# Two attention and MLP layers on one core: the loads of the head on another queue, a second tile centred, the first key product in two parts, and new orders

## The chip, the core and the metric

The kernel runs on one core of one Trainium2 chip. The metric is the device time of one execution in microseconds (us). The same program is timed several times, and the median counts. One execution is also recorded by the hardware profiler.

The core has a matrix engine (TensorE; PE in the profile for the products, PEld for loading the stationary operand), three engines for elementwise work (VectorE is DVE, ScalarE is ACT, GpSimd is POOL) and SyncE (SP), which here only starts transfers. ACT and POOL can start transfers too. Each engine works through its own list of instructions in order, and semaphores make one wait for another.

## What is computed

The input x is 2048 tokens of 512 channels. Two kinds of blocks follow each other twice, each with a residual sum:

```python
x = x + A(layernorm(x))      # linear attention, 32 heads of 16 channels
x = x + B(layernorm(x))      # MLP
# A(x): q, k, v = split(x @ wqkv);  phi(t) = where(t > 0, t + 1, exp(t)) + 1e-6
#   kv = sum over tokens of phi(k) v^T, z = sum over tokens of phi(k), per head
#   out = (phi(q) @ kv) / (phi(q) . z + 1e-6);  return out @ wo
# B(x): y = layernorm(x);  return gelu(y @ w1 + b1) @ w2 + b2      # 512 -> 1792 -> 512
```

Data and weights are bfloat16; the weights are the same in both layers.

## The kernel before

The tokens are cut into 16 tiles of 128 and four chunks of four tiles. A program in Python makes a graph of named operations (class `Graph`). Five lists written out by hand, `CONF["ORDER"]`, one per engine, then set the order in which every engine works through its operations (`Settled.run`, L144). `CONF["PLACES"]` says which slot of which pool (PSUM banks, SBUF buffers) each tile of data takes, and so which earlier user it has to wait for. `CONF["WAY"]` says on which engine some operations run. `assign_waits` (L186) turns the graph into semaphore waits. So the order of the work is that of the lists; the planned durations in the code decide nothing on the chip.

Names, with the layer or tile number behind them:

- Loads: `x0`, `x1` (chunk 0), `xc1` to `xc3` (chunks 1 to 3), `wk0`, `wk1` (two halves of the key weights), `wq`. `CONF["LOADS"]` names each load's queue (L711 to L716). `wv`, `wo`, `w1`, `w2` are loaded by POOL's queue once all transposes of the first norms are done.
- Norm of tile t in block A or B of layer L (`norm`, L757): `stats`, `aggr`, `veps`, `pow` (reciprocal root, on POOL), `nmr`, `norm`. Two tiles of the head have other forms: with `cen` the tile is only centred (`cenA0_0`, L789), goes through TensorE transposes early (`PTC0`, then `tcC0` copies it), and the missing factor is applied as the scale of the exponential (`expk0_0`, `reluk0_0`). With `stat3` set to "act", tile 3 gets its sums from ACT (`sumA0_3`, `sqA0_3`).
- Transposes: `TA`, `TB`, `TP` are DMA transposes issued by SP (L812, L1080); `PTA` with `tcA` are done by TensorE and copied by ACT. In the kernel before, tiles 1, 2 and 3 of the first norm use TensorE (`PTA0_1` to `PTA0_3`).
- Attention: `K`, `Q` (four products of 128 x 512 each), `exp`, `relu`, `min`, `phi` for the feature map, `Z` and `G` (sums over tokens; G is the product of the normed tile with phi(k)), `KV`, `M` (joined with wo), `D`, `ln`, `rec`, `pr`, `pz`, `red`, `den` (denominators), `WO` and `RA` (output and residual sum).
- MLP: `W1`, `gelu`, `W2`, `b2`, `RB` (residual sum). In the last layer `RB1` writes a bfloat16 row block into an output buffer and SP stores it (`OD`). The last tile is done in two halves: columns 0 to 383 (`W21_15_h0`, `RB1_15_0`, `OD15_0`) and 384 to 511 (`W21_15_h1` and so on).

TensorE starts with products on constants (`warm`), while the first loads are under way.

The output buffers are two slots of `outb` (L657). There are ten slots of `yb` for normed tiles and eight of `pkb` for phi(k) (L620).

`attn_k` can already split the key product in two: `halves` (L874) reads the setting `ks`, and with it the parts (2, 3) and (0, 1) of the contraction become two operations, each waiting only for its own half of the weights. No tile of the kernel before sets it.

Of the kernel before, what the change touches and what calls it, by code (L numbers as in the profile page):

```python
# [6 lines left out]
BF16 = mybir.dt.bfloat16  # L7
ACT = mybir.ActivationFunctionType
ALU = mybir.AluOpType

P = 128
# [174 lines left out]
def assign_waits(graph, order, sems, dma_sems):  # L186
# [10 lines left out]
    while len(done) < total:  # L197
        moved = False
        for e in ENGINES:
# [43 lines left out]
    LOADS=[['x0', 'sp', 'x', 0, 0, 1, ''], ['x1', 'sp', 'x', 0, 1, 4, ''], ['wk0', 'sp', 'wk', 0, 0, 2, ''], ['wk1', 'act', 'wk', 0, 2, 4, 'ones'], ['xc1', 'act', 'x', 1, 0, 4, 'x0'], ['xc3', 'act', 'x', 3, 0, 4, ''], ['wq', 'act', 'wq', 0, 0, 4, ''], ['xc2', 'act', 'x', 2, 0, 4, '']],  # L243
    ORDER={
# [39 lines left out]
        "act":  # L284
# [1064 lines left out]
```

## Time and profile before

| | us |
|---|---|
| median of 3 runs | 325.99 (325.9 to 327.17) |
| the profiled execution | 326.31 |
| its span, first to last instruction | 325.1 |
| PE busy | 316.7 (97%) |
| DVE / ACT / POOL busy | 219.3 / 188.9 / 134.9 |
| mean granted TensorE clock | 0.999 |

The profiled execution's time is 1.2 us longer than its span. A busy PE is counted from the first to the modelled end of pipelined products, so idle time of PE is a better sign than its share. The "chain" of the profile goes back from the last instruction, at each step to what released it. Line numbers are those of the kernel before. Landing records and DMA records are the trace's own lists of when each transfer's pieces ran and when its semaphore was raised.

### The profile page before, as it was taken

To read this page: it belongs to the slowest core of one execution; us is meant where nothing else is said; L and a number is where in the kernel's file an instruction comes from. 1 tells how busy PE (TensorE), PEld (TensorE's weight loads), DVE (VectorE), ACT (ScalarE), POOL (GpSimd) and SP (SyncE) were. 2 spreads that over 40 slices of the span, in tenths; PEclk is the share of its full clock that TensorE was granted. 3 is DMA by queue.
4 is the path that set the end of the run, shared out by engine and by line. 5 is a ranking of instruction groups with operands and counts; after the bars stand their busy time and mean duration, and the time that the engine had idled before them with its cause. 6 is when DMAs were issued, how large, how long until landed. Compare 5 with 4: busy or idle time off the path is not lost.

```text
span 325.1 us, 4707 instructions
## 1 busy us (share of the span) xinstructions
PE 316.7 (97%) x1673; PEld 157.2 (48%) x1703; DVE 219.3 (67%) x536; ACT 188.9 (58%) x324; POOL 134.9 (42%) x208
## 2 busy tenths in 40 slices
PE   7899999998999999999999999999999999999997
PEld 3344554665454444444444444558544444444443
DVE  6987799989897496029349899999886843101103
ACT  4799658586675125875982277969824442653220
POOL 6562768793146045001421503976685454000000
PEclk9999999999999999999999999999999999999999
DMA  7734595224011403202101110131143322301002
GB/s 252 188 63 91 139 387 138 43 57 81 11 38 35 90 10 72 49 0 49 34 0 32 34 32 0 26 73 36 33 82 83 69 41 56 79 0 34 16 32 65
DMA packets 51779, 21.55 MB, mean 66 GB/s; under 512 B 46956, under 2 KB 50284, under 8 KB 51756
## 3 DMA queue, kind: packets, MB, share of 16 engines
q1 hardware_dynamic: 49468, 14.18, 20.1%
q0 software_dynamic: 1056, 4.72, 4.2%
q10 hardware_dynamic: 1232, 2.36, 2.2%
q8 instruction: 13, 0.21, 0.3%
q14 instruction: 10, 0.08, 0.1%
HBM read 8.00 MB, written 2.10 MB: 31 GB/s over the span
## 4 chain that ended last, share of the span: by engine, by line
PE 87%; DVE 4%; ACT 3%; DMA 3%; issue 1%; POOL 1%; SPq 0%
PE ps L1177 28%; PE ps L1140 27%; PE ps L879 8%; PE ps L1110 7%; PE ps L896 6%; PE ps L971 4%; PE ps L1000 3%; PE ps L909 2%; DVE xsb L1115 1%; DMA wqkv<-in_A_wqkv_dram 1%; DMA t<-yb 1%; DVE stats L775 1%; PE ps L1163 1%; ACT L1303 1%; ACT gT L1145 1%
## 5 line engine op out<-in xcount | busy, mean ns | idle before, releaser
L1145 ACT ACTIVATE gT<-ps,b1c 128x512 bf16<-128x512 f32 (+1 forms) x140 | 77.2, 601 | 67.2 <-PE ps L1140 66.8
L1140 PE MATMUL ps<-t,w 128*128 128x512 bf16 (+1 forms) x552 | 102.3, 336 | 1.5 <-issue 1.1
L1177 PE MATMUL ps<-w,gT 128*128 128x512 bf16 x425 | 97.6, 379 | 0.5
L1140 PEld LDWEIGHTS ps<-t,w 128*128 128x128 bf16 x560 | 54.6, 98 | 45.5 <-ACT gT L1145 1.6
L1177 PEld LDWEIGHTS ps<-w,gT 128*128 128x128 bf16 x434 | 42.5, 98 | 50.2
L847 ACT ACTIVATE eb<-ps 128x512 bf16<-128x512 f32 x63 | 36.8, 608 | 30.3 <-PE ps L879 15.9
L784 POOL TENSOR_TENSOR rstd<-veps,neghalf 128x1 f32<-128x1 f32 x64 | 38.5, 610 | 22.4 <-DVE veps L782 20.3
L1187 DVE TENSOR_TENSOR outb<-ps,xsb 128x512 bf16<-128x512 f32 x15 | 10.3, 689 | 44.5 <-PE ps L1177 40.1
L879 PE MATMUL ps<-wqkv,t 128*128 128x512 bf16 x125 | 30.6, 379 | 2.2 <-DMA t<-yb 1.1
L775 DVE BATCH_NORM_STATS2 stats<-xsb 128x6 f32<-128x512 f32 x48 | 32.4, 682 | 0.2
L1110 PE MATMUL ps<-gtb,t 128*128 128x512 bf16 x124 | 30.4, 379 | 0.2
L858 ACT ACTIVATE rb<-ps 128x512 bf16<-128x512 f32 x44 | 26.1, 608 | 3.7 <-PE ps L896 2.1
L782 POOL TENSOR_SCALAR veps<-mv 128x1 f32<-128x1 f32 x34 | 7.6, 224 | 48.0 <-DVE mv L777 44.0
L1076 POOL TENSOR_TENSOR t<-t,rr 128x512 bf16<-128x512 bf16 x18 | 19.9, 1114 | 11.3 <-DVE rr L1072 7.6
L798 ACT ACTIVATE yb<-xsb,nmr,rstd 128x512 bf16<-128x512 f32 x21 | 16.9, 811 | 12.9 <-POOL nmr L795 12.5
L896 PE MATMUL ps<-wqkv,t 128*128 128x512 bf16 x95 | 23.6, 379 | 0.1
L1183 DVE TENSOR_TENSOR xsb<-ps,xsb 128x512 f32<-128x512 f32 x16 | 10.8, 679 | 14.7 <-PE ps L1177 14.7
L879 PEld LDWEIGHTS ps<-wqkv,t 128*128 128x128 bf16 x128 | 12.1, 97 | 16.9 <-ACT yb L798 1.5
L1110 PEld LDWEIGHTS ps<-gtb,t 128*128 128x128 bf16 x128 | 12.4, 98 | 14.5 <-issue 0.3
L1064 POOL TENSOR_TENSOR lr<-t,zrow 128x512 f32<-128x512 bf16 x13 | 14.9, 1153 | 9.9 <-ACT zrow L984 3.7
L1126 DVE TENSOR_TENSOR xsb<-xsb,b2b 128x512 f32<-128x512 f32 x20 | 14.4, 730 | 5.2 <-ACT yb L798 5.2
L803 DVE TENSOR_SCALAR yb<-xsb,mv,rstd 128x512 bf16<-128x512 f32 x27 | 15.1, 566 | 3.1 <-POOL rstd L784 2.1
(100 smaller groups left out, 362.1 us busy)
## 6 DMA issues: line engine op xcount, KB each, us to landing
w<-in_B_w_dram POOLq DMA_DIRECT2D x4, 896.0 KB, 9.7
out_dram<-outb SPq DMA_DIRECT2D x15, 128.0 KB, 2.0
t<-in_A_x_dram ACTq DMA_DIRECT2D x3, 512.0 KB, 4.1
t<-yb SPq DMA_TRANSPOSE x61, 2.5
wqkv<-in_A_wqkv_dram ACTq DMA_DIRECT2D x1, 512.0 KB, 5.2
wqkv<-in_A_wqkv_dram POOLq DMA_DIRECT2D x1, 512.0 KB, 4.5
wo<-in_A_wo_dram POOLq DMA_DIRECT2D x1, 512.0 KB, 5.6
t<-in_A_x_dram SPq DMA_DIRECT2D x1, 384.0 KB, 3.1
```

Of the source, the lines that this page charges most:

```text
L775: G.op("dve", lambda e: e.bn_stats(stats[:, s.slot, :], src()), 620, reads=src_keys, writes=[k + "s"], tiles=[s, *src_tiles], name=f"stats ...
L784: G.op("pool", lambda e: e.tensor_tensor(rstd[:, s.slot:s.slot + 1], veps[:, s.slot:s.slot + 1], neghalf[:], op=ALU.pow), 570, reads=[k + ...
L798: G.op("act", lambda e: e.activation(yb[:, y.slot, :], src(), ACT.Identity, bias=nmr[:, s.slot:s.slot + 1], scale=rstd[:, s.slot:s.slot + 1]),
L847: G.op("act", lambda e: e.activation(eb[:, et.slot, :], bank(bt), ACT.Exp, scale=by()), 478, reads=[src_key, *more_keys], writes=[f"e{tag} ...
L858: G.op("act", lambda e: e.activation(rb[:, rt.slot, :], bank(bt), ACT.Relu, scale=by()), 478, reads=[src_key, *more_keys], writes=[f"r{tag ...
L879: ins = e.matmul(bank(b), lhsT=yTa(yT)[:, dt, k * P:(k + 1) * P], rhs=wqkv[:, dt, D:2 * D], start=(i == 0 and n == 0), stop=(i == len(part ...
L896: ins = e.matmul(bank(b), lhsT=yTa(yT)[:, dt, k * P:(k + 1) * P], rhs=wqkv[:, dt, 0:D], start=(dt == 0), stop=(dt == DT - 1))
L1076: lambda e, d=d, tok=tok, heads=heads: e.tensor_tensor(heads(tok()), heads(tok()), rr[:, d.slot, :].unsqueeze(2).broadcast_to([P, H, DH]), ...
L1110: ins = e.matmul(bank(wb), lhsT=yTa(pq)[:, kt, k * P:(k + 1) * P], rhs=gtb[:, kt, :], start=(kt == 0), stop=(kt == DT - 1))
L1140: ins = e.matmul(bank(b, n), lhsT=w1[:, dt, ft * P:(ft + 1) * P], rhs=yTa(yT)[:, dt, k0 * P:k1 * P], start=(dt == 0), stop=(dt == DT - 1))
L1145: G.op("act", lambda e, ft=ft, b=b, k0=k0, k1=k1, n=n: e.activation(gT[:, g.slot, ft * 512 + k0 * P:ft * 512 + k1 * P], bank(b, n), ACT.Ge ...
L1177: ins = e.matmul(bank(b), lhsT=gT[:, g.slot, ft * 512 + k * P:ft * 512 + (k + 1) * P], rhs=w2[:, ft, :], start=(ft == 0), stop=(ft == FT - 1))
```

## The change

Settings, orders and buffers change; the arithmetic does not.

- `LOADS`: `xc3`, `wq` and `xc2` are issued by SP instead of ACT. On SP they stand behind `x0 x1 wk0 TA0_0` (with `TA0_1` between `wq` and `xc2`). `wk1` and `xc1` stay with ACT.
- `cen1`: tile 1 is centred too and goes through TensorE transposes as `PTC1`, `tcC1`. Its normed form, used by Q and G, is transposed by DMA (`TA0_1` on SP), in place of `PTA0_1`, `tcA0_1`.
- `ks0`: the first key product becomes `K0_0a` (halves 2, 3 of the weights, from `wk1`) and `K0_0b`.
- The last layer's outputs use the ten slots of `yb`; `outb` goes, and `pkb` grows from 8 to 10 slots.
- All five orders and all places are written anew. `W21_15_h0` and `RB1_15_0` now come before `W21_15_h1` and `RB1_15_1`, with `RB1_10` still between the two additions.
- `WAY`: in layer 0, `b20_0` to `b20_2` go from POOL to DVE and `b20_7` to `b20_13` from DVE to POOL; in layer 1, `b21_1`, `b21_3`, `b21_4` go to POOL, `b21_0`, `b21_13` to DVE; some 20 `pr` and `pz`, some 30 `veps` and four `za` change sides between DVE and POOL, among them `pz0_1_0` to POOL, `vepsA0_0` and `vepsA0_2` to DVE.

```diff
-    LOADS=[..., ['xc3', 'act', 'x', 3, 0, 4, ''], ['wq', 'act', 'wq', 0, 0, 4, ''], ['xc2', 'act', 'x', 2, 0, 4, '']],
+    LOADS=[..., ['xc3', 'sp', 'x', 3, 0, 4, ''], ['wq', 'sp', 'wq', 0, 0, 4, ''], ['xc2', 'sp', 'x', 2, 0, 4, '']],
         "sp":
-            "x0 x1 wk0 TA0_0 TA0_4 TA0_5 TA0_7 TA0_13 TA0_6 TA0_12 TA0_14 TA0_15 TA0_8 TA0_9 TA0_10 TA0_11 b1 Tb1 b2 TP0_1_3 "
-            "TP0_1_1 TP0_1_0 TP0_1_2 TB0_0 TB0_1 TB0_2 TB0_3 TB0_7 TP0_2_1 TB0_6 TB0_4 TB0_5 TP0_2_0 TP0_2_2 TP0_2_3 TA1_0 "
...
-            "OD15_1 OD10 OD15_0",
+            "x0 x1 wk0 TA0_0 xc3 wq TA0_1 xc2 TA0_4 TA0_5 TA0_7 TA0_6 TA0_13 TA0_12 TA0_14 TA0_15 TA0_8 TA0_10 TA0_9 TA0_11 "
+            "b1 Tb1 TP0_1_3 TP0_1_1 TP0_1_0 TP0_1_2 TB0_0 TB0_1 b2 TB0_2 TB0_3 TP0_2_1 TB0_4 TB0_7 TB0_5 TB0_6 TP0_2_2 "
...
+            "OD11 OD12 OD8 OD9 OD15_0 OD10 OD15_1",
         "pe":
-            "warm0 warm7 warm6 warm5 PTC0 warm4 warm3 warm2 warm8 warm1 K0_0 PTA0_2 PTA0_1 K0_2 PTA0_3 K0_1 G0_0_0 K0_3 "
-            "Q0_0_2 Q0_0_0 K0_4 Q0_0_1 G0_1_0 G0_2_0 K0_5 G0_3_0 K0_7 Z0_0 G0_4_0 K0_13 K0_6 Q0_1_3 Q0_1_0 G0_5_0 Q0_1_2 "
...
-            "W21_11_7 W21_8_7 W21_9_0 W21_9_7 W21_10_7 W21_15_h1 W21_15_h0",
+            "warm0 warm8 warm4 warm7 warm5 PTC0 warm3 warm2 warm6 warm1 K0_0a K0_0b PTC1 PTA0_2 K0_1 PTA0_3 K0_2 G0_0_0 K0_3 "
+            "G0_1_0 Q0_0_2 Q0_0_1 Q0_0_0 K0_4 Q0_1_0 K0_5 G0_2_0 G0_3_0 G0_4_0 K0_7 Q0_1_3 K0_6 Z0_0 G0_5_0 K0_13 Q0_1_2 "
...
+            "W21_8_7 W21_9_0 W21_9_7 W21_10_7 W21_15_h0 W21_15_h1",
         "act":
-            "wk1 xc1 sumA0_3 tcC0 xc3 sqA0_3 wq tcA0_2 expk0_0 tcA0_1 reluk0_0 expk0_2 tcA0_3 expk0_1 xc2 reluk0_1 expk0_3 "
+            "wk1 xc1 sumA0_3 tcC0 sqA0_3 expk0_0 tcC1 tcA0_2 reluk0_0 expk0_1 tcA0_3 reluk0_1 expk0_2 reluk0_2 reluk0_3 "
...
         "dve":
-            "ones statsA0_0 aggrA0_0 cenA0_0 statsA0_2 aggrA0_2 statsA0_1 aggrA0_1 vepsA0_1 normA0_2 normA0_0 normA0_1 "
+            "ones statsA0_0 aggrA0_0 vepsA0_0 cenA0_0 statsA0_2 normA0_0 aggrA0_2 statsA0_1 vepsA0_2 aggrA0_1 cenA0_1 "
+            "vepsA0_1 normA0_2 statsA0_4 normA0_3 mink0_0 normA0_1 aggrA0_4 phik0_0 statsA0_7 mink0_1 statsA0_5 phik0_1 "
...
-        NT4, NYB, NPK, NER, NGT, NLR, NSTAT, NOUT = 12, 10, 8, 4, 2, 2, 12, 2
+        NT4, NYB, NPK, NER, NGT, NLR, NSTAT = 12, 10, 10, 4, 2, 2, 12
...
-        outb = SB("outb", [P, NOUT, D], BF16)
...
-                ot = Tile(OUT, f"out{st}")
-                G.op("dve", lambda e: e.tensor_tensor(outb[:, ot.slot, :], bank(b), xsb[:, st, :], op=ALU.add), 600,
+                ot = Tile(YB, f"out{st}")
+                G.op("dve", lambda e: e.tensor_tensor(yb[:, ot.slot, :], bank(b), xsb[:, st, :], op=ALU.add), 600,
```

In the part of TensorE's order between the first attention and the first MLP, `Q0_3_1` no longer stands ahead of `KV0_0`, nor `Q0_3_0` ahead of `WO0_0_0`; `Q0_2_3` does instead. Three Q products rather than two stand between the `WO0` products. Before the first product on chunk 1 (`W10_1`), `W10_0_8_1` and `W10_0_11_1` are new; they stood some units later.

More of the change, by code (lines that the diff above doesn't have):

```diff
@@ L242 @@
     WARM=[[512, 512, 512, 512, 512, 512, 512], [256], [256], [256], [256], [256], [256], [256], [256]],
-    LOADS=[['x0', 'sp', 'x', 0, 0, 1, ''], ['x1', 'sp', 'x', 0, 1, 4, ''], ['wk0', 'sp', 'wk', 0, 0, 2, ''], ['wk1', 'act', 'wk', 0, 2, 4, 'ones'], ['xc1', 'act', 'x', 1, 0, 4, 'x0'], ['xc3', 'act', 'x', 3, 0, 4, ''], ['wq', 'act', 'wq', 0, 0, 4, ''], ['xc2', 'act', 'x', 2, 0, 4, '']],
+    LOADS=[['x0', 'sp', 'x', 0, 0, 1, ''], ['x1', 'sp', 'x', 0, 1, 4, ''], ['wk0', 'sp', 'wk', 0, 0, 2, ''], ['wk1', 'act', 'wk', 0, 2, 4, 'ones'], ['xc1', 'act', 'x', 1, 0, 4, 'x0'], ['xc3', 'sp', 'x', 3, 0, 4, ''], ['wq', 'sp', 'wq', 0, 0, 4, ''], ['xc2', 'sp', 'x', 2, 0, 4, '']],
     ORDER={
         "sp":
[38 rows of a table removed]
-        "act":
[31 rows of a table removed]
-        "dve":
[42 rows of a table removed]
-        "pool":
[16 rows of a table removed]
[38 rows of a table added]
+        "act":
[30 rows of a table added]
+        "dve":
[42 rows of a table added]
+        "pool":
[16 rows of a table added]
     },
@@ L671, in build_kernel @@
         STATS = Pool("stats", NSTAT)
-        OUT = Pool("out", NOUT)
         psum = Pool("psum", 8)
@@ L1168, in mlp_down @@
                          tiles=[hb, g], name=f"W2{L}_{st}_h{h}", lat=MM_DRAIN, n=FT)
-                    G.op("dve", lambda e, hb=hb, cs=cs, n=n: e.tensor_tensor(outb[:, ot.slot, cs], bank(hb, n), xsb[:, st, cs], op=ALU.add),
+                    G.op("dve", lambda e, hb=hb, cs=cs, n=n: e.tensor_tensor(yb[:, ot.slot, cs], bank(hb, n), xsb[:, st, cs], op=ALU.add),
                          60 + n * 1.06, reads=[f"w{L}_{st}_{h}", ("x", st)], writes=[f"out{st}_{h}"], tiles=[hb, ot], name=f"RB{L}_{st}_{h}", lat=60)
-                    dma("sp", lambda e, cs=cs: e.dma_start(rows(out_dram, c)[:, k, cs], outb[:, ot.slot, cs]), [f"od{st}_{h}"],
+                    dma("sp", lambda e, cs=cs: e.dma_start(rows(out_dram, c)[:, k, cs], yb[:, ot.slot, cs]), [f"od{st}_{h}"],
                         tiles=[ot], reads=[f"out{st}_{h}"], name=f"OD{st}_{h}", sem=f"d_out_h{h}", kb=n // 4)
@@ L1185, in mlp_down @@
             else:
-                ot = Tile(OUT, f"out{st}")
-                G.op("dve", lambda e: e.tensor_tensor(outb[:, ot.slot, :], bank(b), xsb[:, st, :], op=ALU.add), 600,
+                ot = Tile(YB, f"out{st}")
+                G.op("dve", lambda e: e.tensor_tensor(yb[:, ot.slot, :], bank(b), xsb[:, st, :], op=ALU.add), 600,
                      reads=[f"w{L}_{st}", ("x", st)], writes=[f"out{st}"], tiles=[b, ot], name=f"RB{L}_{st}", lat=40)
-                dma("sp", lambda e: e.dma_start(rows(out_dram, c)[:, k, :], outb[:, ot.slot, :]), [f"od{st}"], tiles=[ot],
+                dma("sp", lambda e: e.dma_start(rows(out_dram, c)[:, k, :], yb[:, ot.slot, :]), [f"od{st}"], tiles=[ot],
                     reads=[f"out{st}"], name=f"OD{st}", sem=("out", ot), kb=128)
```

514 rows, old and new, of tables (ORDER, PLACES, WAY) are left out of this document.

## The prediction

> **What bounds the kernel now.** I read the page's shares first, then busy time by stretches, then the chain that ended last, then the timelines of the places where TensorE stands still. TensorE bounds it:
>
> ```profile
> PE 316.7 (97%) x1673; PEld 157.2 (48%) x1703; DVE 219.3 (67%) x536; ACT 188.9 (58%) x324; POOL 134.9 (42%) x208
> PE 87%; DVE 4%; ACT 3%; DMA 3%; issue 1%; POOL 1%; SPq 0%
> ```
>
> The second line is the chain's share by engine. The change adds and removes no matrix product (TA0_1's four PE transposes become PTC1's four). So only TensorE's gaps, its end and new gaps can move the time. Busy time by stretch (us: PE, PEld, DVE, ACT, POOL, clock, DMA share, GB/s) shows where they are:
>
> ```profile
> 6.00:9.00 3.00, 2.44 (x16) 1.26 (x17) 2.67 (x10) 1.79 (x5) 1.97 (x6) 1.00 0.98 326
> 12.00:15.00 3.00, 1.94 (x10) 0.73 (x9) 3.00 (x13) 2.39 (x4) 2.00 (x5) 1.00 0.87 232
> 15.00:18.00 3.00, 3.00 (x14) 1.36 (x15) 2.70 (x9) 1.95 (x4) 1.67 (x7) 1.00 0.22 44
> 76.00:80.00 4.00, 3.27 (x26) 2.35 (x24) 4.00 (x7) 2.40 (x6) 0.36 (x1) 1.00 0.56 101
> ```
>
> TensorE is full from 15 us on, at full clock, but for one hole before 80. In order of time, the chain names what ends last (start, us, what):
>
> ```profile
> 1.71 4.47 DMA wqkv<-in_A_wqkv_dram
> ...
> 10.60 4.26 DMA t<-yb
> ...
> 79.41 1.02 issue
> ```
>
> K0_0 waits for wk0 (6.18), K0_4 for the transpose TA0_4 (14.86), and W10_1_5_0 stands at 79.4. From here each 512-column product costs 0.216 us by its weight loads (K0_3 to Q0_0_2: 0.86 for four); I call four a unit.
>
> **The head, first tiles.** In the new order DVE puts vepsA0_0 (0.15) ahead of cenA0_0 (4.19 before, now 4.26), so tcC0 on ACT ends at about 5.75 instead of 5.63. K0_0a needs only wk1, landed at 5.78 by the landing records: it starts at 5.82, K0_0b at 6.25 (wk0 6.18), and K0_0 is done at about 6.87 instead of 7.28. expk0_0, at 8.04 because ACT first sat behind PTA0_2 (idle 1.21), starts at 6.93. cenA0_1 (0.35, the row of cenA0_0) is the added DVE work; its cover is gone, since DVE is 2.67 of 3 busy there, and normA0_2 slips from 6.43 to 7.03. PTC1 follows at 6.9, tcC1 at 7.5 to 8.1 behind expk0_0, so K0_1 starts at 8.16, where K0_2 started at 8.20. Then PTA0_3 (0.26) at 9.02, K0_2 at 9.28, G0_0_0 at 10.14, K0_3 at 11.0. Up to here nothing is won but G0_1_0's input: reluk0_1 ends at 11.0, phik0_1 at 11.46, against 14.26 before, because both first tiles now come early. So G0_1_0 runs at 11.87 and Q0_0_2 at 12.73.
>
> **The moved loads.** ACT gains nothing from losing them: with xc3's issue between tcC0 and sqA0_3, these start 0.49 us apart, the usual pitch.
>
> ```profile
> 5.04 0.60 ACT L835 ACTIVATE t<-ps 128x512 bf16<-128x512 bf16 x1
> 5.04 0.33 ACTq L702 DMA_DIRECT2D t<-in_A_x_dram  x1
> 5.50 0.39 ACTq L708 DMA_DIRECT2D wqkv<-in_A_wqkv_dram  x1
> 5.53 0.71 ACT L770 ACTIVATE eb<-t,stats 128x512 bf16<-128x512 bf16 x1
> ```
>
> On SP they stand behind waits. TA0_0 now issues at 5.6 (normA0_0 moves up) and takes 1.28 of SP; xc3 then goes at 6.95 and wq at 7.35 (0.4 each, instead of 5.04 and 5.50). TA0_1 waits for normA0_1 (about 8.9) and goes at 9.0; behind it xc2 at 10.3; behind that TA0_4, which waits for normA0_4 (about 11.9). 512 KB moved in about 1.6 us of full DMA share (xc3's packets 6.5 to 8.2). So xc3 moves about 8.0 to 9.6, wq to 11.3, TA0_1's 128 KB to 12.2 (landed 12.7), xc2 to 13.8, TA0_4 to 14.7 (landed 15.2). x tiles 8 to 15 are read later than that; wq is needed at 12.73. Q0_0_2 therefore meets TA0_1 on the spot.
>
> K0_4 comes after Q0_0_1 and Q0_0_0, at 15.33. It started at 14.99 with two units fewer done. The gain is 2 x 0.864 - 0.38 = 1.35 us if TA0_4 has landed by then. No row shows a transpose queued behind a load on its own queue, so I bound it: alone a transpose takes 2.5 us (61 of them), beside loads on the other queue 4.1 to 4.3. With 4.3 from 11.93, TA0_4 lands at 16.2 and the gain is 0.4; with 2.5 it lands at 14.4 and the gain stays 1.35. I take 1.1, near the upper end, because xc2 is issued 1.6 us ahead of TA0_4 instead of 0.23.
>
> [...]
>
> Does the lead survive? ACT is 3.00 of 3 busy from 18 to 21 and DVE from 21 to 24, but ACT idles 2.6 us and DVE 4.8 us in all between 15 and 38, mostly waiting for TensorE. Following banks and queues in the new order, K0_5 needs TA0_5 (about 16.4, used at 17.1) and K0_11 comes at about 32.6 instead of 33.7. I carry -1.1.
>
> **To the first MLP.** One Q unit fewer stands ahead of WO0_0 and one more behind it; pz0_1_0 (0.69) goes from DVE to POOL, where 1.13 us of idle time before pr0_0_3 takes most of it. So the residual sums start earlier still, and ten units of PE cover the way to TB0_1 instead of nine. Cost 0; if POOL were late here, up to 0.7.
>
> **The hole at 79.** W10_1_5_0 waits for TB0_5, issued at 76.02, which takes 4.3 us instead of 2.5. The DMA records show why: a 16 KB packet of the instruction queue occupies one engine from 77.93 for 1.36 us, and the last sixteenth of TB0_5 lands at 80.34. The hole is 1.36 us of TensorE. In the new order W10_0_8_1 and W10_0_11_1 (0.44 each) stand ahead of the first W10_1, and the last transpose is TB0_6, about as late as TB0_5 was. [...] Gain between 0 and 1.36; I take 0.9.
>
> [...]
>
> **The rest.** b20, b21, pz, pr and veps change sides; over the whole DVE program the kinds I count by median pitch fall from 201 to 199 us, and TensorE's units per stage are the same or one apart. Before, TensorE loses three further waits of 0.2 to 0.4 us (at 194, 208 and 217); new ones of that size will come. I charge 0.2, between -0.5 and +1.5.
>
> **The end.**
>
> ```profile
> 321.33 0.29 DVE L1169 TENSOR_TENSOR outb<-ps,xsb 128x128 bf16<-128x128 f32 x1 [1.92 <-DMA out_dram<-outb]
> 321.80 0.69 DVE L1187 TENSOR_TENSOR outb<-ps,xsb 128x512 bf16<-128x512 f32 x1 [0.18 <-DMA out_dram<-outb]
> 322.69 0.56 DVE L1169 TENSOR_TENSOR outb<-ps,xsb 128x384 bf16<-128x384 f32 x1 [0.20 <-PE ps L1163]
> ```
>
> Ten buffers end the waits for outb, but the last addition waits for TensorE either way. The halves change places: the last addition falls from 0.56 to 0.29, yet RB1_10 (0.69) stands between the two and the 128 KB store OD10 is issued at about 322.9 instead of 322.52. Between 0 and -0.35; I take -0.15.
>
> **Sum.** The profiled execution took 326.31 (span 325.1), 0.3 above the median. -1.1 - 0.9 + 0.2 - 0.15 = -1.95: 324.36 for it, **324.0** on the median of 325.99.
>
> **Rivals.**
> 1. *One term pays, not both.* The instruction packet hits in full, or DVE, full at 12 to 15, hands the head's lead back. Then about 0.9 to 1.2 is won: 324.9 to 325.3. For it: DVE 3.00 of 3; against it: its idle time after 16.
> 2. *Slower: SP's queue.* If a transpose behind a load starts only when that load has landed, TA0_1 lands at 11.8 + 2.5 = 14.3 and TA0_4 at 15.9 + 2.5 = 18.4. Q0_0_2 stalls 1.6 us and K0_4 another 1.5: 3.1 - 1.35 = 1.75 lost in the head. With the hole at 79 kept and 0.2 of new waits the time is 327.8. It decides from TA0_1 landing after 14.1. Against it: x0, x1 and wk0 ran on from one another on SP's queue.
> 3. *The change does nothing:* the starts win and new waits eat them, 326.0.
>
> **Chances.** Forecast 0.55 (a quarter of it above 324.36, the bound of 0.5%, which is about what a measurement of this kernel can tell), rival 1 0.27 (a fifth of it below that), rival 2 with other new waits 0.13, rival 3 0.05. Faster 0.42 + 0.05 = 0.47, same 0.40, slower 0.13. Range: down to -3.1 (head 1.35, hole 1.36, end 0.35), 322.9; up to 326.9, which leaves out most of rival 2.
>
> **What would show it.** Right: K0_4 at 15.2 to 15.6 with Q0_0_1 before it, TA0_1 landing near 12.7, no PE idle time over 0.5 us after 16, RB1_15_1 last at 0.29. Wrong: Q0_0_2 or K0_4 waiting over 1 us for t<-yb; a hole near 78 before the first W10_1; PE waiting for K0 banks between 20 and 33; DVE or POOL ending waits of TensorE near 54 or 205.

## The result, and the profile after

The changed kernel took 324.35 us in the median of 9 executions (323.99 to 325.34), the kernel before 325.90 us on the same chip (9 executions, 325.40 to 327.65). The ratio is 0.9947, with a 95% interval from 0.9933 to 0.9961: 0.53% or about 1.7 us faster. The forecast was 324.0 with a range from 322.9 to 326.9. The profiled execution took 324.26 us (span 323.0) against 326.31 (span 325.1) before: 2.05 us less, where the sum of the prediction had 1.95. Five executions of two experiments below (two with the loads on ACT's queue, three with the loads alone) ran at a granted clock of 0.995, and by the means without them, the 2.0 us and the 1.8 us found there are 1.7 and 1.3 us.

The two lines of the profile's page, busy time and the chain's share by engine:

```profile
PE 318.4 (99%) x1703; PEld 157.5 (49%) x1703; DVE 216.9 (67%) x528; ACT 189.8 (59%) x324; POOL 145.6 (45%) x217
PE 92%; DVE 3%; POOL 2%; ACT 1%; DMA 1%; issue 0%
```

TensorE still bounds the kernel; the chain's share of DMA and "issue" fell from 4% to 1%. Busy time by stretch, in the stretches shown before and one that is new (us: PE, PEld, DVE, ACT, POOL, clock, DMA share, GB/s):

```profile
6.00:9.00 3.00, 2.53 (x17) 1.08 (x16) 2.78 (x11) 2.53 (x6) 2.00 (x4) 1.00 0.74 208
12.00:15.00 3.00, 3.00 (x15) 1.29 (x14) 3.00 (x10) 2.34 (x5) 2.48 (x6) 1.00 0.82 205
15.00:18.00 3.00, 3.00 (x15) 1.36 (x14) 2.83 (x10) 2.97 (x7) 2.58 (x6) 1.00 0.49 99
49.50:53.00 3.50, 3.13 (x16) 1.23 (x15) 3.50 (x7) 3.02 (x8) 2.28 (x3) 1.00 0.24 49
76.00:80.00 4.00, 4.00 (x30) 2.72 (x28) 3.93 (x9) 2.52 (x7) 0.70 (x1) 1.00 0.01 4
```

TensorE is now full from 12 to 18 us (from 12 to 15 it had 1.94 of 3 before) and from 76 to 80 (3.27 of 4 before). From 49.5 to 53 it is not, which the prediction did not have. The timeline of TensorE (start, busy, ..., in brackets the idle time before and what ended it) shows the head in its new order:

```profile
5.81 1.02 PE L876 MATMUL ps<-wqkv,t 128*128 128x512 bf16 x4 [0.31 <-ACT t L832]
8.10 1.04 PE L876 MATMUL ps<-wqkv,t 128*128 128x512 bf16 x4 [0.30 <-ACT t L832]
...
11.79 1.03 PE L968 MATMUL ps<-pkb,yb 128*128 128x512 bf16 x4
12.65 2.76 PE L906 MATMUL ps<-t,wqkv 128*128 128x512 bf16 x12
15.25 1.03 PE L876 MATMUL ps<-wqkv,t 128*128 128x512 bf16 x4
```

The lines are `K0_0a` with `K0_0b`, `K0_1`, `G0_1_0`, the three Q units and `K0_4` (its first record, a weight load, is at 15.10). Before, `K0_4` started at 14.96 with two units fewer done.

Where the 2.0 us of the span went, from TensorE's idle time by stretches. It is counted by units: from the first weight load of one unit to that of the next, less the ideal time of the products between them.

| stretch (us, by each kernel's own clock) | predicted | measured |
|---|---|---|
| up to 15.3: the head | -1.1 | -1.44 (4.64 to 3.20) |
| 62 to 82: the hole | -0.9 | -1.27 (1.50 to 0.23) |
| 49.5 to 62 | in +0.2 | +0.55 (0.25 to 0.80) |
| all else | in +0.2 | -0.17 |
| TensorE's end to the span's end | -0.15 | +0.18 (2.41 to 2.58) |

The measured terms add up to -2.15, the span fell by 2.04, so a term is good to about 0.1. The experiments below ask which of these terms belong to the change, and which to the one execution that was recorded.

### The profile page after: what moved, and what is told of

It is laid out like the page before. It is cut to its first block, busy times and chain, and to the rows that moved or that the text cites. A ratio compares the mean times of both kernels' runs of the same rounds, so it can differ in the third digit from the quotient of the medians.

```text
span 323.0 us, 4748 instructions
## 1 busy us (share of the span) xinstructions
PE 318.4 (99%) x1703; PEld 157.5 (49%) x1703; DVE 216.9 (67%) x528; ACT 189.8 (59%) x324; POOL 145.6 (45%) x217
## 4 chain that ended last, share of the span: by engine, by line
PE 92%; DVE 3%; POOL 2%; ACT 1%; DMA 1%; issue 0%
PE ps L1137 30%; PE ps L1174 29%; PE ps L876 9%; PE ps L1107 8%; PE ps L893 5%; PE ps L997 4%; PE ps L906 2%; PE ps L968 2%; DMA t<-in_A_x_dram 1%; POOL lr L1061 1%; POOL t L1092 1%; PE ps L1160 1%; PE ps L951 1%; POOL w L725 1%; DVE rd L1064 0%; DVE eb L848 0%
## 5 line engine op out<-in xcount | busy, mean ns | idle before, releaser
L844 ACT ACTIVATE eb<-ps 128x512 bf16<-128x512 f32 x62 | 36.1, 602 | 25.9 <-PE ps L876 10.9
L1184 DVE TENSOR_TENSOR yb<-ps,xsb 128x512 bf16<-128x512 f32 x15 | 10.2, 685 | 43.9 <-PE ps L1174 43.9
L1107 PE MATMUL ps<-gtb,t 128*128 128x512 bf16 x128 | 31.6, 379 | 0.4 <-DVE gtb L984 0.4
L876 PE MATMUL ps<-wqkv,t 128*128 128x512 bf16 x128 | 31.1, 379 | 0.6 <-ACT t L832 0.6
L855 ACT ACTIVATE rb<-ps 128x512 bf16<-128x512 f32 x43 | 25.3, 600 | 3.1 <-PE ps L893 2.1
L779 POOL TENSOR_SCALAR veps<-mv 128x1 f32<-128x1 f32 x36 | 10.6, 295 | 36.0 <-DVE mv L774 30.8
L1061 POOL TENSOR_TENSOR lr<-t,zrow 128x512 f32<-128x512 bf16 x17 | 20.1, 1182 | 10.7 <-DVE t L850 4.9
L893 PE MATMUL ps<-wqkv,t 128*128 128x512 bf16 x96 | 24.1, 379 | 0.0
L1123 POOL TENSOR_TENSOR xsb<-xsb,b2b 128x512 f32<-128x512 f32 x17 | 19.9, 1181 | 4.9 <-DVE yb L800 4.7
L800 DVE TENSOR_SCALAR yb<-xsb,mv,rstd 128x512 bf16<-128x512 f32 x27 | 14.4, 533 | 9.7 <-POOL rstd L781 9.5
L1073 POOL TENSOR_TENSOR t<-t,rr 128x512 bf16<-128x512 bf16 x14 | 14.9, 1070 | 12.1 <-DVE rr L1069 10.9
L1107 PEld LDWEIGHTS ps<-gtb,t 128*128 128x128 bf16 x128 | 12.5, 98 | 15.1 <-DVE gtb L984 0.9
```

Source lines behind the costliest of these rows:

```text
L844: G.op("act", lambda e: e.activation(eb[:, et.slot, :], bank(bt), ACT.Exp, scale=by()), 478, reads=[src_key, *more_keys], writes=[f"e{tag} ...
L855: G.op("act", lambda e: e.activation(rb[:, rt.slot, :], bank(bt), ACT.Relu, scale=by()), 478, reads=[src_key, *more_keys], writes=[f"r{tag ...
L876: ins = e.matmul(bank(b), lhsT=yTa(yT)[:, dt, k * P:(k + 1) * P], rhs=wqkv[:, dt, D:2 * D], start=(i == 0 and n == 0), stop=(i == len(part ...
L893: ins = e.matmul(bank(b), lhsT=yTa(yT)[:, dt, k * P:(k + 1) * P], rhs=wqkv[:, dt, 0:D], start=(dt == 0), stop=(dt == DT - 1))
L1061: lambda e, r=r, tok=tok: e.tensor_tensor(lr[:, r.slot, :], tok(), zrow[:], op=ALU.mult), 1150 if on_pool else 600,
L1107: ins = e.matmul(bank(wb), lhsT=yTa(pq)[:, kt, k * P:(k + 1) * P], rhs=gtb[:, kt, :], start=(kt == 0), stop=(kt == DT - 1))
```

## The experiments

Ratios are against the kernel before, timed on the same chip as each kernel; differences in us are differences of ratios times 326. Waits are TensorE's, and "by units" is the count explained above. Edits are shortened; `...` marks what is left out.

**The loads on ACT's queue again.**

```diff
-['xc3', 'sp', ...], ['wq', 'sp', ...], ['xc2', 'sp', ...]
+['xc3', 'act', ...], ['wq', 'act', ...], ['xc2', 'act', ...]
-"sp": x0 x1 wk0 TA0_0 xc3 wq TA0_1 xc2 TA0_4 ...
+"sp": x0 x1 wk0 TA0_0 TA0_1 TA0_4 ...
-"act": wk1 xc1 sumA0_3 tcC0 sqA0_3 expk0_0 tcC1 tcA0_2 reluk0_0 expk0_1 ...
+"act": wk1 xc1 sumA0_3 tcC0 xc3 sqA0_3 wq expk0_0 tcC1 tcA0_2 reluk0_0 expk0_1 xc2 ...
```

> The changed kernel, but xc3, wq and xc2 are issued by ACT again, after tcC0, sqA0_3 and expk0_1 as in the kernel before; everything else stays. My theory: the moved loads carry nothing of the gain; ACT's issues cost its stream no time, and wq's data only has to be there at 12.65 us. The loads start about 2 us earlier, TA0_0 lands later (near 11 us instead of 8.04, needed at 9.9 for G0_0_0 at the earliest by no one: K0_4's tiles count), Q0_0_2 starts at 12.6 to 12.9, K0_4 at 15.0 to 15.5, the time stays within 0.3 us of the changed kernel (324.1 to 324.7). Rival A: the gain of the head comes from a freed ACT queue: then tcC1 or expk0_1 comes 0.5 us or more later, K0_1 starts after 8.6 instead of 8.10, and 0.5 to 1.1 us are lost (324.9 to 325.5). Rival B: the loads on SP delay the transposes behind them: then TA0_1 and TA0_4 land over 0.5 us earlier here and the time falls by 0.3 or more.

Measured: 326.88 us, ratio 1.0009 (0.9977 to 1.0042). Without the moved loads the change brings nothing that can be told from noise; they are worth 0.62%, about 2.0 us, and my theory that they carry nothing fell. None of the rivals had the cause either. The chain of waits of this kernel (start, us, what) and TensorE's timeline:

```profile
8.65 0.84 ACT t L827 x2
...
9.93 6.25 DMA t<-yb
...
16.23 2.76 PE ps L901 x12
```

```profile
16.23 1.04 PE L901 MATMUL ps<-t,wqkv 128*128 128x512 bf16 x4 [2.32 <-DMA t<-yb]
```

`TA0_1` is issued at 9.93 and lands at 16.18; `Q0_0_2` stands for it (2.71 us by units). In that execution `x1` also landed at 5.60 instead of 4.33 and, through `sumA0_3` ahead of `tcC0` on ACT, held the head up by another 1.1 us, so the kernel was profiled a second time.

> The kernel with xc3, wq and xc2 issued by ACT once more, for a second profile. In the first, TA0_0 (issued 6.66) landed at 13.83, 0.96 us after wq, TA0_1 (issued 9.94) at 16.18, and Q0_0_2 waited 2.71 us. Theory: a transpose that is issued while loads of the other queue move doesn't land before these have landed, and TA0_1 comes 2.3 to 2.5 us behind TA0_0 on the same queue. Then TA0_0 lands 0.5 to 1.0 us after wq again, TA0_1 2.2 to 2.6 us after TA0_0, and Q0_0_2 waits 1.5 to 3 us. Rival (the first was chance: x1 landed at 5.60 there instead of 4.34 to 4.80): with x1 before 4.9, TA0_1 lands before 13.5 and Q0_0_2 waits less than 1 us.

Measured, one execution: 325.32 us, with `x1` at 4.43. The wait is there without the late `x1`:

```profile
14.26 2.76 PE L901 MATMUL ps<-t,wqkv 128*128 128x512 bf16 x12 [1.02 <-DMA t<-yb]
```

It is 1.41 us by units, just under what I had written, and `TA0_1` came 1.93 us after `TA0_0` instead of 2.2 to 2.6. The landing records of the kernels side by side (issue to landing):

| | TA0_0 | wq landed | TA0_1 |
|---|---|---|---|
| changed kernel | 5.54 to 8.04 | 11.97 | 9.00 to 12.61 |
| changed kernel, second profile | 5.53 to 8.03 | 12.19 | 8.92 to 12.85 |
| loads on ACT | 6.66 to 13.83 | 12.87 | 9.93 to 16.18 |
| loads on ACT, second profile | 5.52 to 12.29 | 12.21 | 8.83 to 14.22 |
| kernel before | 7.19 to 11.28 | 10.72 | |

With the loads on the other queue, `TA0_0` lands 0.1 to 1.0 us after `wq`, and `TA0_1`, behind it on SP's queue, a further 1.9 to 2.4 us later. On one queue `TA0_0`, issued ahead of the loads, is through in 2.5 us (2.5 to 3.2 in all nine profiles that have these loads behind it on SP, the experiments below included), and `TA0_1`, behind `wq`, lands 0.6 to 0.7 us after it.

The edit changes two things at once, the queue and the order. On SP the loads can't be issued before the issue of `TA0_0` has ended, at 6.84; on ACT `xc3` went out ahead of `TA0_0`, and `wq` 0.1 and 0.2 us after the start of `TA0_0`'s issue. The record points to the order. In all 14 profiles of this case, `TA0_0`, `TA0_1` and `TA0_4` landed at least 0.08 us after every load that was issued before their own issue ended, on either queue: in the changed kernel `TA0_0` comes 0.62 us after `xc1` of ACT's queue. And in the five profiles in which ACT issued `xc2` after `TA0_0`'s issue had ended, `TA0_0` landed 1.4 to 2.9 us ahead of `xc2`. No run issues these loads from ACT behind `TA0_0`, so queue and order were not taken apart by an experiment.

In the second profile with the loads on ACT, no packet of `TA0_0` moved between the end of its issue (6.80) and 8.4 us; then, from 8.4 to 10.3, 512 did, as many as a transpose has, beside 244 of ACT's queue (DMA rows of that stretch; `q1` is SP's queue; packets, MB, share of the engines' time):

```profile
q10 hardware_dynamic: 244, 0.30, 76.3%
q1 hardware_dynamic: 512, 0.13, 36.5%
```

Yet it landed at 12.29, 2 us after its last data and 0.08 after `wq`. So what was late is the start and, above all, the landing; why it landed so late no trace shows.

**The loads alone, in the kernel before.**

```diff
-"sp": x0 x1 wk0 TA0_0 TA0_4 ...
+"sp": x0 x1 wk0 TA0_0 xc3 wq xc2 TA0_4 ...
```

> The kernel before with the moved loads alone: xc3 and wq issued by SP behind TA0_0, xc2 behind wq and ahead of TA0_4; ACT issues wk1 and xc1 only. Theory A (the loads are worth something by themselves, since transposes and loads on one queue don't share the DMA engines' time): TA0_0, which took 4.1 us beside the loads of ACT's queue, lands within 3 us of its issue at 7.2, TA0_4 lands no later than 14.9, and 0.3 to 1 us come off. Theory B (mine): the loads help only a kernel that needs TA0_1 early. Here they go out 3 us later (behind TA0_0, about 8.5 and 8.9), wq lands at 12.8 to 13.4 instead of 10.72, Q0_0_2 starts 1.0 to 1.5 us later than 11.82, half of that disappears in the wait of 1.42 us ahead of K0_4, and the time is 0.2 to 0.8 us longer than before.

Measured: 327.96 us, ratio 1.0055 (1.0033 to 1.0077), some 1.8 us slower than before: theory B's direction, and more than its 0.2 to 0.8. `TA0_0` was fast (7.25 to 9.77), as theory A has it, but that did not help: `wq`, issued at 9.21, landed at 14.15.

```profile
14.20 1.90 PE L903 MATMUL ps<-t,wqkv 128*128 128x512 bf16 x8 [1.37 <-DMA wqkv<-in_A_wqkv_dram]
```

So the same edit costs 1.8 us in the one order and saves 2.0 in the other. The difference that the traces show is where the first transpose stands: at 5.5 us in the changed kernel (`normA0_0` was moved up on DVE), at 7.2 in the kernel before, and the loads start behind it. No run moved `normA0_0` alone, so that this is what decides is argued.

**Without the centring of tile 1.**

```diff
-"pe": ... K0_0b PTC1 PTA0_2 K0_1 ...
+"pe": ... K0_0b PTA0_2 PTA0_1 K0_1 ...
-"sp": ... wq TA0_1 xc2 ...
+"sp": ... wq xc2 ...
-"dve": ... cenA0_1 vepsA0_1 normA0_2 statsA0_4 normA0_3 mink0_0 normA0_1 ...
+"dve": ... vepsA0_1 normA0_2 normA0_1 statsA0_4 normA0_3 mink0_0 ...
```

ACT's and POOL's orders follow it (`tcA0_1` behind `tcA0_2` in place of `tcC1`, `powA0_1` two places earlier).

> The changed kernel without the centring of the second tile: normA0_1 after normA0_2, its transpose on TensorE from the normalised tile (PTA0_1) as in the kernel before, no cenA0_1, no TA0_1 on SP. My theory: centring is what pays in the head; without it K0_1 starts 0.6 to 1.1 us later than 8.10, the two units that were ahead of K0_4 shrink, TensorE's idle time up to 15.3 us rises from 3.20 by 0.5 to 1.1 us, and the time is 324.9 to 325.4. Rival: the head is set by the landing of wq (11.97) and the transposes, so the gap only moves behind G0_0_0, and the time stays within 0.3 us of the changed kernel.

Measured: 325.67 us, ratio 0.9972 (0.9955 to 0.999); the interval overlaps that of the changed kernel (up to 0.9961) at its edge; the difference is 0.25%, 0.8 us. `K0_1` starts at 9.06 instead of 8.10, behind the whole norm of tile 1:

```profile
9.06 1.04 PE L870 MATMUL ps<-wqkv,t 128*128 128x512 bf16 x4 [0.69 <-ACT t L826]
```

The start is as the theory had it (0.6 to 1.1 us later).

**The first key product in one piece.**

```diff
-"pe": ... warm1 K0_0a K0_0b PTC1 ...
+"pe": ... warm1 K0_0 PTC1 ...
```

> The changed kernel with the first key unit in one piece again (K0_0 instead of K0_0a and K0_0b). My theory: the pair is worth at most the time between the landings of wk1 and wk0, 0.1 to 0.7 us in the profiles so far, and most of it is lost behind it, since K0_1 waits for tcC1 on ACT and Q0_0_2 for TA0_1, which don't depend on K0_0 by more than its end: K0_0 starts at wk0's landing, the time is 0 to 0.3 us longer than that of the changed kernel. Rival: expk0_0, the first of ACT's queue behind K0_0, comes later by the full amount and with it tcC1 and K0_1: then 0.3 to 0.7 us are lost.

Measured: 324.93 us, ratio 0.9960 (0.9944 to 0.9976), 0.4 us above the changed kernel, but the intervals overlap over most of their length. `wk1` and `wk0` landed at 6.24 and 6.42 here, so the pair had 0.2 us to win in this execution, 0.4 in that of the changed kernel (5.67, 6.03). Its worth, 0 to 0.5 us, is not settled.

**The hole at 79: the kernel before with a longer instruction stream.**

```diff
-WARM[0] = [512] * 7
+WARM[0] = [128] * 28
```

> The kernel before with one edit: the first warm-up product list is 28 products of 128 columns instead of 7 of 512 columns (the same columns and the same output, 21 more pairs of weight load and product, so that the instruction stream of TensorE is 42 instructions longer ahead of everything else, at the same work). My theory: the hole of 1.36 us ahead of W10_1_5_0 is there because a 16 KB packet of TensorE's instruction queue (77.93 us, 1.36 us long) hits one DMA engine while it moves TB0_5 (issued 76.02, landed 80.34). With the stream 42 instructions longer the packets come about 3 us earlier, the one near 78 comes at 74 to 76, TB0_5 takes about 2.5 us, and the hole shrinks to under 0.3 us: 1.0 to 1.4 us come off the time. Rival A: the fetch has nothing to do with it; TB0_5 takes 4 us again and the time stays within 0.3 us. Rival B: the packet hits TB0_6 or another transpose instead, with a like hole at another place; the time stays within 0.5 us.

Measured: 326.19 us, ratio 0.9993 (0.9974 to 1.0012). The mechanism is right: the packet came at 73.61, even earlier than expected, `TB0_5` took 2.48 us, and the hole is gone.

```profile
76.00:80.00 4.00, 3.95 (x31) 2.91 (x31) 4.00 (x7) 2.57 (x7) 0.52 (x1) 1.00 0.49 98
```

But the time did not fall by 1.0 to 1.4 us: that price held for one execution, not for the median. Part of the gain is lost behind the span. The span of the profiled execution was 324.0, 1.1 less than before, while its time lay 2.84 us above its span instead of 1.2, and this trace alone has a 14th instruction packet, at 325.75 us, after the span's end (the 13 other profiles have 13); that the execution waited for it is likely, not shown. Over all executions the mean span is 324.8 against 325.1 before. A second profile of the kernel before shows one reason why the median did not move.

> The kernel before, unchanged, for a second profile. If the hole at 79 comes from an instruction packet that happens to meet TB0_5, it need not be there each time: packets of the same rank came up to 2 us apart in the profiles of kernels with the same order so far. With the packet within 76.0 to 78.5 the hole is 0.8 to 1.4 us, outside of that below 0.3 us. If the hole is there with the packet elsewhere, the fetch is not its cause. Q0_0_2 starts at 11.5 to 12.5 and K0_4 at 14.7 to 15.7 in either case.

Measured, one execution: 326.04 us (span 324.8). There is no hole at 79 (the packet came at 79.65, after `TB0_5` had landed at 78.74), but one of 0.85 us ahead of the first MLP, where a packet at 60.36 met `TB0_1` (59.58 to 62.82). And `Q0_0_2` waited 1.50 us, since `TA0_0` took 5.9 us beside ACT's loads:

```profile
13.19 1.90 PE L909 MATMUL ps<-t,wqkv 128*128 128x512 bf16 x8 [1.11 <-DMA t<-yb]
...
62.87 0.83 PE L1140 MATMUL ps<-t,w 128*128 128x256 bf16 x6 [0.57 <-DMA t<-yb]
```

The hole's absence is what I had expected for a packet outside 76.0 to 78.5. My expectation for `Q0_0_2` (11.5 to 12.5) missed: it was 13.19.

**cpm0_2 earlier.** In the profile of after, `WO0_0_2` waits 0.74 us for `cpm0_2`. DVE's and POOL's timelines in that stretch:

```profile
49.34 1.32 DVE L848 TENSOR_SCALAR eb<-eb 128x512 bf16<-128x512 bf16 x1
50.58 0.67 DVE L1064 TENSOR_REDUCE rd<-lr 128x32 f32<-128x512 f32 x1
51.17 0.67 DVE L984 TENSOR_SCALAR gtb<-ps 128x512 bf16<-128x512 f32 x1
```

```profile
49.34 1.17 POOL L1092 TENSOR_TENSOR t<-t,lr 128x512 bf16<-128x512 bf16 x1
```

`minq0_2_0` (L848), 0.28 us in the profiles where it is not held up, takes 1.32 beside POOL's product, and `cpm0_2` (L984) is queued behind it.

```diff
-"dve": ... den0_1_0 minq0_2_0 red0_1_2 cpm0_2 ...
+"dve": ... den0_1_0 cpm0_2 minq0_2_0 red0_1_2 ...
```

> The changed kernel with one step moved on DVE: cpm0_2 stands right behind den0_1_0, ahead of minq0_2_0. My theory: WO0_0_2's wait of 0.74 us at 51.2 to 51.9 is there only because minq0_2_0 took 1.32 us beside POOL's pr0_0_1 and cpm0_2 was queued behind it; cpm0_2 now ends by about 50.2, the wait goes, and 0.5 to 0.74 us come off: 323.6 to 323.9 by the side of 324.35. Rival: what is late next (normB0_1 and its transpose TB0_1, behind the same DVE queue) takes the wait over, TensorE stands for the same 0.7 us before the first MLP, and the time stays within 0.2 us.

Measured: 324.32 us, ratio 0.9931 (0.9905 to 0.9957), not told apart from the changed kernel. The wait of `WO0_0_2` was gone, and in the profiled execution another stood in its place:

```profile
61.86 0.50 PE L1131 MATMUL ps<-t,w 128*128 128x256 bf16 x3 [0.55 <-DMA t<-yb]
```

That one (0.93 us by units) is for `TB0_1`, 57.83 to 61.82, with an instruction packet at 59.70. So rival and measurement agree in the time, but for another reason than the rival gave: `normB0_1` was no later.

**The last stores in another order.**

```diff
-"dve": ... RB1_15_0 RB1_10 RB1_15_1
+"dve": ... RB1_10 RB1_15_0 RB1_15_1
-"sp": ... OD9 OD15_0 OD10 OD15_1
+"sp": ... OD9 OD10 OD15_0 OD15_1
```

> The changed kernel with the last additions in another order: RB1_10 and its store OD10 ahead of RB1_15_0 and OD15_0. My theory: the stretch from TensorE's end to the end of the span (2.56 us) is set by the store queue: OD15_1 lands 1.72 us after its issue at 321.26, which comes 0.2 us after the end of its addition because OD10's issue stands in front of it on SP. With OD10 out of the way OD15_1 is issued at 321.1 at the latest and 0.1 to 0.4 us come off. Rival: OD15_0, now issued behind OD10 and last but one, lands as late as OD10 did; the time stays within 0.15 us.

Measured: 323.79 us, ratio 0.9920 (0.9891 to 0.9950), by the ratio alone not told apart from the changed kernel. But from the start of `W21_15_h1` to the landing of `OD15_1` it took 2.95 us (319.46 to 322.41) instead of 3.64 (319.34 to 322.98): 0.69 us less, more than the 0.1 to 0.4 expected. The issues of the last stores by SP, in the changed kernel and here:

```profile
320.28 0.33 SPq L1168 DMA_DIRECT2D out_dram<-yb  x1
320.88 0.33 SPq L1186 DMA_DIRECT2D out_dram<-yb  x1
321.26 0.43 SPq L1168 DMA_DIRECT2D out_dram<-yb  x1
```

```profile
320.40 0.85 SPq L1162 DMA_DIRECT2D out_dram<-yb  x2
```

`OD15_1` is issued 1.46 us after the unit's start instead of 1.92, and lands 1.49 after its issue instead of 1.72, with no 128 KB store just ahead of it.

**Both moves.**

> The changed kernel with both moves: cpm0_2 behind den0_1_0, and RB1_10 and OD10 ahead of RB1_15_0 and OD15_0. In the first single look at cpm0_2's move the wait of 0.74 us of WO0_0_2 was gone, and W10_0_6_0 waited 0.93 us for TB0_1 instead, which took 4.0 us while an instruction packet came at 59.70. Theory A (the new wait was chance): with the packet outside 57 to 60.5 here, TB0_1 takes 2.5 us, no wait over 0.3 us stands between 49.5 and 62, and the time is 0.5 to 0.7 us below the version with the moved stores alone (its ratio to before was 0.992). Theory B (the packet comes at a place in the stream that now falls on TB0_1): TB0_1 takes 3.8 us or more again and the time is that of the version with the moved stores, within 0.2 us.

Measured: 323.70 us, ratio 0.9913 (0.9891 to 0.9936): the fastest version of this case, 0.87% below the kernel before, and 0.34% below the changed kernel with intervals that just overlap. No wait over 0.3 us stands between 49.5 and 62; the packet came at 60.45, 0.17 us after `TB0_1` had landed. So the event of theory A came and the time of theory B: against the version with the stores alone the gain is 0.07%, about 0.2 us, and the 0.5 us that theory A gave to the missing wait did not come. The next profile says why.

**The changed kernel once more.**

> The changed kernel, unchanged, for a second profile. Theory: a slow transpose on TensorE's path is a matter of where TensorE's instruction packets fall; an instruction packet of 0.9 us or more between 57.7 and 60.2 would cost up to 1 us ahead of W10_0_6_0, one outside of it nothing, and none can stand ahead of the first W10_1 any more, whose last transpose lands near 76. The wait of WO0_0_2 for cpm0_2 is no chance: 0.7 to 0.8 us again, with minq0_2_0 at 1.2 to 1.4 us beside POOL's product. Q0_0_2 starts at 12.5 to 13.4.

Measured, one execution: 323.95 us. The wait of `WO0_0_2` that I had called no chance is not there. Again DVE and POOL:

```profile
49.57 0.28 DVE L848 TENSOR_SCALAR eb<-eb 128x512 bf16<-128x512 bf16 x1
...
50.37 0.68 DVE L984 TENSOR_SCALAR gtb<-ps 128x512 bf16<-128x512 f32 x1
```

```profile
49.58 1.29 POOL L1092 TENSOR_TENSOR t<-t,lr 128x512 bf16<-128x512 bf16 x1
```

In the trace's nanoseconds `minq0_2_0` starts 4 ns ahead of POOL's product here and takes 0.28; in the first profile it starts 2 ns behind it and takes 1.32. Over the seven profiles of kernels with these two steps in this place, DVE was the slow one in two (2 ns behind in both), POOL in five (in four DVE was 4 to 10 ns ahead, in one 2 ns behind), POOL's product taking 1.29 or 1.30 instead of 1.17. A tie is broken by nanoseconds, about as fine as the records tell, and 1 us hangs on it.

**wq ahead of xc3.**

```diff
-"sp": x0 x1 wk0 TA0_0 xc3 wq TA0_1 xc2 TA0_4 ...
+"sp": x0 x1 wk0 TA0_0 wq TA0_1 xc3 xc2 TA0_4 ...
```

> The version with cpm0_2 and the last stores moved, and on SP the order TA0_0, wq, TA0_1, xc3, xc2, TA0_4 (xc3 from ahead of wq to behind TA0_1). Theory (transposes and loads of one queue move in the order of issue): TA0_1 no longer has 512 KB of xc3 ahead of it and lands at 11.4 to 12.0 instead of 13.08, the wait of Q0_0_2, 0 to 0.5 us in the profiles so far, is gone, TA0_4 lands as before (14.7 to 15.2), and the time is 0 to 0.4 us below 323.70. Rival: xc3 now lands at about 13.5 to 14 instead of 11.05, the statistics of tile 15 on DVE (13.04) wait for it and normA0_5 and mink0_2 behind them come late: Q0_1_0, K0_4 or K0_5 wait 0.3 to 1 us and the time rises by as much.

Measured: 324.85 us, ratio 0.9967 (0.995 to 0.9985), 0.5% slower than the version it was made from. `TA0_1` landed at 11.87, as the theory of order on one queue gives it, but the same order put a whole megabyte ahead of `TA0_4`, which landed at 16.86, 0.47 after `xc2`:

```profile
17.00 1.02 PE L870 MATMUL ps<-wqkv,t 128*128 128x512 bf16 x4 [0.98 <-DMA t<-yb]
```

"TA0_4 lands as before" was the theory's mistake: `xc3`, now behind `TA0_1` on SP, is not issued before 10.56, and the time in which it moved before is lost. The rival had the size of the new wait (0.3 to 1 us), by another path, the statistics of tile 15. (This execution also met an instruction packet: `TB0_1` took 4.1 us, and W10_0_6_0 waited 1.04.)

## Why the prediction was right, step by step

- **Head.** The starts were foretold to within 0.36 us (in brackets the first weight load as measured): `K0_0a` 5.82 (5.78), `PTC1` 6.9 (6.84), `K0_1` 8.16 (8.10), `G0_1_0` 11.87 (11.57), `Q0_0_2` 12.73 (12.65), `K0_4` 15.33 (15.10), `K0_11` 32.6 (32.24). `K0_0a` was released by `tcC0` on ACT, not by `wk1`, which had landed at 5.67. The lead survives as said: `K0_11` is 1.46 us earlier, and 1.49 in the pair of second profiles (33.97 and 32.48). The term was sized at 1.1 because a transpose behind a load had no row and I let it take up to 4.3 us; `TA0_4` took 3.19, `TA0_1` 3.60.
- **The moved loads.** `TA0_1` landed at 12.61 against 12.7 (0.63 after `wq`, landed at 11.97). The 12.7, and the 15.2 for `TA0_4`, put SP's transfers one behind the other, which was an estimate; in the profile of the changed kernel they did land in the order of their issue: `TA0_0` 8.04, `xc3` 10.55, `wq` 11.97, `TA0_1` 12.61, `xc2` 14.50, `TA0_4` 14.99. What the sum did not see is what the move is for: with the loads left on ACT, `TA0_1` lands 1.4 to 3.6 us later, and no gain is left that could be measured. I had the 4.1 us of `TA0_0` beside ACT's loads in a row and used it as a bound for `TA0_4`, not as the price of the alternative. Rival 2 had the sign of this mechanism the wrong way round: here a transpose behind a load on its own queue waited less than one that the other queue's loads held up (issue to landing 3.6 and 3.9 us for `TA0_1` behind `wq`, 7.2 and 6.8 for `TA0_0` beside ACT's loads).
- **The hole at 79.** Right in cause, wrong in one step. `TB0_6`, the last transpose now, is not "about as late as TB0_5 was": it lands at 76.05, 2.65 us ahead of the first `W10_1` (78.70), so the new order takes the hole away fully (-1.27). The 0.9 was an estimate, near the 0.88 us of the two units put ahead of it, for a packet that hits again; no run shows a packet tied to one place in the order. Over the eight profiles with the changed kernel's order of TensorE, the one near 60 us came 26.7 to 29.6 us after the start of `K0_11`, when 339 to 358 of TensorE's weight loads had started, and the one near 79, the one that made the hole before, 44.7 to 46.7 us after it, at 468 to 478. That makes the hole of the kernel before a matter of chance: it cost 1.36 and, with the loads alone, 1.24 in two profiles and nothing in the second profile of the kernel before. Five profiles of this case show 0.85 to 1.36 us of TensorE's time for one such packet. A median holds only a part of it, which may be why the medians differ by 1.55 us and the profiles by 2.05.
- **New waits.** +0.2 was charged, +0.38 measured in the one profile (0.55 - 0.17), most of it the tie at 49.3. This is the one sign named ahead that failed: TensorE stood for 0.74 us at 51, where no wait over 0.5 was to come after 16. Without the tie (second profile) the stretch holds 0.22 us instead of 0.86, counting single gaps above 0.05.
- **The end.** The mis-sized term with the wrong sign: the last addition fell to 0.28 us as said, but the end is set by the store's issue and landing, and the sum priced only the addition. It was +0.18 instead of -0.15, and taking `OD10` out from between showed 0.69 us that can be had there.
- **The parts don't add up.** The loads alone cost 1.8 us; all the rest without the loads is worth nothing that could be measured (1.0009); together they give 1.7. Of the rest, centring is worth some 0.8 given the loads. The buffers, the steps that changed engines and the new order for the hole were not run by themselves; that the hole is gone is shown by the traces alone.
- **Luck.** That the sum came within 0.1 us of the profiled execution is in part luck: the head and the hole together brought 0.7 us more than forecast, the new waits and the end cost 0.5 us more, and two of these terms, the hole and the tie, change from one execution to the next.

## What to carry to other kernels

Where a transpose is on the critical path, let the large loads be issued behind it (here its own queue saw to that) rather than just ahead of it or beside it on another one (with the loads on ACT's queue `TA0_1` landed 1.4 to 3.6 us later), but only if the transpose goes out early enough not to hold the loads back; the same edit was a gain of 2.0 us in one order and a loss of 1.8 in the other. Before paying for a hole in a profile, take a second profile: the time that this kernel lost to an instruction packet (0.85 to 1.36 us) or to a tie between two engines (1.04 us) was a lottery ticket, and the cure is slack ahead of TensorE's need (`TB0_6` landed 2.65 us ahead of it, and the hole was gone), not a move of that one step. At the end of a kernel order the last stores so that nothing stands between the last result and its store (0.69 us here).

## What the runs showed of the hardware that was not expected

**Instruction packets and transposes.** Of the transposes that TensorE waits for next, those in flight while a 16 KB packet of the instruction queue ran took 3.2 to 4.4 us, the others 2.5 (landing and DMA records). Transposes that nothing waits for at once meet packets too, in every profile: in the changed kernel `TA0_6`, issued at 16.58, took 3.98 us with a packet at 18.51.

| kernel | transpose | took | packet at (length) | wait |
|---|---|---|---|---|
| before | TB0_5, 76.02 to 80.34 | 4.32 | 77.93 (1.36) | 1.36 |
| before, second profile | TB0_1, 59.58 to 62.82 | 3.24 | 60.36 (0.93) | 0.85 |
| before, loads moved | TB0_5, 77.02 to 81.39 | 4.37 | 79.08 (1.21) | 1.24 |
| cpm0_2 earlier | TB0_1, 57.83 to 61.82 | 3.99 | 59.70 (1.08) | 0.93 |
| wq ahead | TB0_1, 59.04 to 63.14 | 4.10 | 61.06 (0.98) | 1.04 |
| before, longer stream | TB0_5, 76.60 to 79.08 | 2.48 | 73.61 (1.18) | none |
| changed kernel | TB0_1, 57.72 to 60.22 | 2.50 | 60.27 (1.57) | none |
| changed kernel, second profile | TB0_1, 57.24 to 59.74 | 2.50 | 61.98 (0.93) | none |

**DVE beside POOL.** In the five profiles compared (both of before, the changed kernel, cpm0_2 earlier, both moves), every `min` of 512 bf16 columns on DVE (L848, L857 and the like) that started with 0.2 us or more of a 512-column operation of POOL still to go lasted until 0.15 to 0.16 us after POOL's end: 1.32 us with 1.17 left, 0.93 with 0.78, 0.71 with 0.56, 0.53 with 0.38. Beside POOL's one-column operations (`veps`, `pow`, `nmr`) it took 0.26 to 0.32, much as with nothing beside it (0.23 to 0.30). The longest of these waits is that of the tie above, where DVE lost 1.04 us. Why the 512-column operations hold `min` up and the one-column ones do not, 0.56 us long as `pow` is, no trace shows.
